# Attention output in eight narrow products side by side, and its row sums through 32x32 transposes on VectorE

## The chip, the cores and the metric

The kernel runs on one core of a Trainium2 chip. The metric is the device time of one launch in microseconds. Before the change it is 1025.22 us, the median of three runs (1023.84 to 1025.31).

The core's engines run beside each other, each through its own queue of instructions: TensorE multiplies matrices, VectorE and ScalarE work elementwise and read what TensorE leaves in PSUM, GpSimd adds, SyncE issues most of the transfers. In the profile TensorE appears as PE (products) and PEld (loading of the stationary operand), VectorE as DVE, ScalarE as ACT, GpSimd as POOL, SyncE as SP.

## What is computed

A linear attention without softmax for 8 batches, 8 heads, 576 tokens and 64 dimensions a head; its output is divided by its root mean square over the 64 dimensions; then follows an MLP with a leaky ReLU on the 4608 x 512 matrix x that the heads side by side make. The weights w_in and w_out are float64 in memory, the rest is float32.

```python
kv  = einsum('bhsd,bhse->bhde', k, v)
out = einsum('bhsd,bhde->bhse', q, kv)
rms = sqrt(mean(out * out, axis=-1, keepdims=True) + 1e-06)
a   = out / rms * g_norm
x   = a.transpose(0, 2, 1, 3).reshape(4608, 512)
h   = x @ w_in                     # 512 x 2048
return maximum(0.01 * h, h) @ w_out  # 2048 x 512
```

## The kernel before

**Order of the work.** The 4608 tokens make nine blocks of 512. Attention goes by batches of 576 tokens, so that each batch falls into two stretches that end at block borders (448 and 128 tokens for batch 1, 384 and 192 for batch 2, up to 64 and 512 for batch 7). `first_attention` (L316) computes kv of batch 0 and its first 512 tokens, in two halves of 256. `first_block` (L515) runs the MLP of block 0 in 16 plain rounds of h (4 products of 512 columns) and o_acc (4 products of 512 columns); between them `between` (L555) starts the rest of batch 0 (64 tokens), the steps of batch 1, and loads and rounds the float64 weights. Then the loop at L570 runs the blocks 1 to 8, each in four chunks of `product_h` (L445) and `product_o` (L478). These are Strassen products: seven products of halves for four quarter results. One of the seven is four matmuls of 256 columns and shows in the trace as a row "x8", since each float32 matmul is two records. After two of the products of each `product_h` and `product_o`, `go(a_steps, 1)` puts in one step of the attention of the next batch: 16 places a block.

**Who sets the order.** TensorE's order is the order of the program (`matmul`, L84, pins each). What SyncE loads and the rounding of weights is pinned too. VectorE and ScalarE get their order from the scheduler of the framework, which puts an instruction where its inputs are ready by its own reckoning; on the chip that order is fixed.

**The attention of one batch** (`attention`, L297). Four steps, one for each pair of heads: q is transposed by VectorE in 32x32 blocks (L303), and kv of both heads of the pair is multiplied into the PSUM tile kv_ps (L250). Then `copy_kv` (L253) copies kv into `kvs`, a tile that was zeroed once (L140): for each pair p and each e of 4 there are 32 columns, 16 of one head and 16 of the other, and the rows of the other head are zero. So one product over 128 rows serves both heads. Then for each stretch four steps of `outputs` (L262) and one of `divide` (L277):

- `outputs` for one e: four products, one for each pair, 128 rows to 32 output rows each, side by side in one PSUM tile o_ps; ScalarE reads it twice, once squared into sq (L270), once times g into x[:, e] (L271); VectorE adds the squares up (L274).
- `divide`: one matmul with `same`, a matrix of ones in 16x16 blocks on the diagonal (L223 to L228), adds the squares over the 16 rows of a head into ss_ps and spreads the sum over them (L280); ScalarE takes the root (L282), VectorE the reciprocal (L283) of all n columns, and multiplies x by it (L284).

The PSUM tiles of these steps come from the pool ps_att with two buffers ("att"). The MLP uses the other six banks as h_a, h_b, h_c, o_a, o_b, o_c. The product that accumulates into a bank waits until VectorE or ScalarE has read it; the closest such pairs have one other product between them: 7 and 4 in `product_h`, 6 and 7 as well as 7 and 4 in `product_o`. VectorE's adds for this are at L373 (`add`).

**The order of rows in x.** Row p of x[:, e] is row 4p + e of the transposed x, so w_in is read as "(p e) f -> p e f" (L191) with one DMA for each piece of 128 columns (L164).

Of the kernel before, what the change touches and what calls it, by code (L numbers as in the profile page):

```python
# [11 lines left out]
AF = mybir.ActivationFunctionType  # L12
ALU = mybir.AluOpType
# [8 lines left out]
def kernel(  # L22
# [27 lines left out]

    nc = tc.nc
# [4 lines left out]
    E = P // H  # L56
# [11 lines left out]
    assert H * D == DM and S == 64 * (J + JJ) and E * NE == D and B * S == NB * NT  # L68
# [89 lines left out]

    def load_f64(src):
        a, n = src.shape[1:]  # L160
        n //= 2
        pool, tag = next(raw_homes)
        raw = pool.tile([P, a * n, 2], U32, tag=tag, name="raw")
        pin(nc.sync.dma_start(raw.rearrange("p (a n) two -> p a (n two)", a=a), src))  # L164
        return raw
# [25 lines left out]
    w_in_e = w_in.rearrange("(p e) f -> p e f", e=NE)  # L191
    w_jobs = []
    for c in range(NC):
        for h in range(2):
            for u in range(U):
                f0 = h * (DF // 2) + (c * U + u) * P
                w_jobs += [(w1_sb[h][c][:, u], w_in_e[:, :, f0:f0 + P]),
                           (w2_sb[h][c][:, u:u + 1, :], w_out[f0:f0 + P].unsqueeze(1))]
# [4 lines left out]
    def load_w(j):  # L203
# [3 lines left out]
        else:  # L207
            nc.sync.dma_start(dst, src)

    def round_w(j):  # L210
        if w_in.dtype == I64:
# [10 lines left out]

    same = consts.tile([P, H, E], F32, name="same")  # L223
    nc.gpsimd.memset(same, 1.0)
    nc.gpsimd.affine_select(same, same, pattern=[[-E, H], [0, E]], base=0, channel_multiplier=1,
                            compare_op=ALU.is_ge, fill=0.0)
    nc.gpsimd.affine_select(same, same, pattern=[[E, H], [0, E]], base=E - 1,
                            channel_multiplier=-1, compare_op=ALU.is_ge, fill=0.0)  # L228


    g_sb = consts.tile([P, NE], F32, name="g_sb")
    for h in range(H):
        pin(nc.gpsimd.dma_start(g_sb[h * E:(h + 1) * E], g_norm.rearrange("(i e) -> i e", e=NE)))

# [18 lines left out]
    def copy_kv(b, ps, kv_ps):  # L253
        for l in range(2):
            r = slice(64 * l, 64 * l + 64)
            nc.vector.tensor_copy(kvs[b % 2][r, ps, :, l, :],
                                  kv_ps[r, ps].rearrange("p a (i e) -> p a e i", e=NE))

    def t2k(n, name):
        return work.tile([P, n], F32, tag="t2k", name=name, bufs=4)  # L260

    def outputs(b, lo, hi, e, sums, o_ps, new=t2k):  # L262

        i, n = lo // NT, hi - lo
        x = block(i)[:, :, lo - i * NT:hi - i * NT]
        for p in range(NP):
            matmul(o_ps[32 * p:32 * p + 32, :], lhsT=kvs[b % 2][:, p, e, :, :],
                   rhs=qTs[b][:, p, lo - b * S:hi - b * S], start=True, stop=True)
        sq = new(n, "sq")
        nc.scalar.activation(sq, o_ps, func=AF.Square)  # L270
        nc.scalar.activation(x[:, e, :], o_ps, func=AF.Copy, scale=g_sb[:, e:e + 1])  # L271
        if sums is None:
            return sq
        nc.vector.tensor_add(sums, sums, sq)  # L274
        return sums

    def divide(lo, hi, sums, ss_ps, new=t2k):  # L277
        i, n = lo // NT, hi - lo
        x = block(i)[:, :, lo - i * NT:hi - i * NT]
        matmul(ss_ps, lhsT=same.rearrange("p h e -> p (h e)"), rhs=sums, start=True, stop=True)  # L280
        rms = new(n, "rms")
        nc.scalar.activation(rms, ss_ps, func=AF.Sqrt, scale=1.0 / D, bias=eps_sb)  # L282
        nc.vector.reciprocal(rms, rms)  # L283
        nc.vector.tensor_mul(x, x, rms.unsqueeze(1).to_broadcast([P, NE, n]))  # L284
# [31 lines left out]
    def first_attention():  # L316
# [4 lines left out]
        def keep_warm(n=1):  # L321
            for _ in range(n):
                matmul(idle, lhsT=kvs[1][:, 0].rearrange("p e l i -> p (e l i)"),
                       rhs=kvs[1].rearrange("p a e l i -> p (a e l i)"), start=True, stop=True)
# [30 lines left out]
        free = iter(("ob", "hb", "hc", "oa", "oc", "ha", "ob", "hb", "hc", "oa"))  # L355

        def ps(name):
            return ps_m.tile([P, N2], F32, tag=next(free), name=name)

        sums = [None, None]  # L360
        for e in range(NE):
            sums[0] = outputs(0, 0, N2, e, sums[0], ps("o_ps"), spare)
        sums[1] = outputs(0, N2, NT, 0, None, ps("o_ps"), spare)
        divide(0, N2, sums[0], ps("ss_ps"), spare)
        for e in range(1, NE):
            sums[1] = outputs(0, N2, NT, e, sums[1], ps("o_ps"), spare)
        divide(N2, NT, sums[1], ps("ss_ps"), spare)
# [183 lines left out]
    steps = {6 + i: tail for tail in [tail_of(0, NT, S)] for i in range(NE + 1)}  # L551
    steps.update((i, a1) for a1 in [attention(1)] for i in (12, 13, 16, 17, *range(18, 29)))
# [73 lines left out]
```

## Time and profile before

| | |
|---|---|
| median of three runs | 1025.22 us |
| the profiled execution | 1025.05 us, its span 1023.3 us |
| mean granted TensorE clock | 0.997 |
| PE busy | 1001.4 us, 98% of the span |
| DVE, ACT, POOL busy | 424.4, 262.6, 505.0 us |
| o_ps products, of 64 to 512 columns | 544 records, 68 steps |
| ss_ps products | 34 records, 17 steps |

The page gives the busy time of each engine, the chain of work that ended last, and the costliest groups of instructions with their mean duration. The timeline lists instructions in order of time, merged where they follow each other: start, length, engine, line, operation, output and inputs, shape, number; in brackets the idle time of the engine before it and what ended it. All matmuls have line L85, the helper; what they do is told by the tile that they write. The end of a matmul is modelled and overlaps the next one, so costs on TensorE are best read from start to start. The waits list says who waited for whom, in total, how often, and the longest.

### The profile page before, as it was taken

The numbers are of one execution on the slowest core, as the hardware profiler recorded it, in microseconds if no ns is written. First come the engines' busy times: TensorE is split into PE (matmuls) and PEld (weight loads), VectorE is DVE, ScalarE is ACT, GpSimd is POOL, SyncE is SP. The second block draws the span as 40 slices with busy tenths as digits, with TensorE's granted clock in tenths as the row PEclk, the third lists the DMA queues.
The fourth block names the chain that finished last, engine by engine and source line by source line (L and its number), as shares of the span: only waits on it lengthen the run. The fifth ranks groups of instructions, "written<-read, shape, count | busy, mean of one in ns | idle before, by whom it ended". The sixth has DMA issues, their size and how long they took to land.

```text
span 1023.3 us, 13007 instructions
## 1 busy us (share of the span) xinstructions
PE 1001.4 (98%) x5164; PEld 773.2 (76%) x5164; DVE 424.4 (41%) x591; ACT 262.6 (26%) x497; POOL 505.0 (49%) x403
## 2 busy tenths in 40 slices
PE   8799999999999999999999999999999999999997
PEld 4444336778887788878888788878887888888886
DVE  2896681235323533156313722354323521332222
ACT  2653432322123211322132212221222112112210
POOL 2000212555655655556555655564555566666641
PEclk9899999999999999999999999999999999999999
DMA  9598404300340016000520043002100010001001
GB/s 226 200 292 224 131 0 125 102 0 1 92 134 1 1 53 174 1 1 1 164 62 1 1 118 108 1 1 76 58 1 1 1 42 1 1 1 42 1 1 41
DMA packets 45309, 63.41 MB, mean 62 GB/s; under 512 B 5312, under 2 KB 39104, under 8 KB 45248
## 3 DMA queue, kind: packets, MB, share of 16 engines
q1 hardware_dynamic: 34560, 51.95, 18.5%
q10 hardware_dynamic: 10432, 10.62, 3.3%
q8 instruction: 41, 0.67, 0.3%
q14 instruction: 20, 0.16, 0.1%
q0 software_dynamic: 256, 0.00, 0.0%
HBM read 53.12 MB, written 9.44 MB: 61 GB/s over the span
## 4 chain that ended last, share of the span: by engine, by line
PE 91%; DVE 4%; DMA 2%; SPq 1%; issue 1%; ACT 0%; DVEq 0%; ACTq 0%
PE o_a L85 21%; PE h_a L85 21%; PE h_c L85 11%; PE o_c L85 10%; PE o_b L85 5%; PE h_b L85 5%; PE h_ps L85 5%; PE o_acc L85 5%; PE o_ps L85 3%; PE kv_ps L85 2%; DVE rms L283 2%; PE ss_ps L85 1%; DMA k_in<-in_k_dram 1%; DVE sq L274 1%; DMA early_kv<-in_v_dram 1%
## 5 line engine op out<-in xcount | busy, mean ns | idle before, releaser
L85 PE MATMUL o_a<-wt,gs 128*128 128x256 f32 x512 | 124.8, 386 | 2.9 <-DVE o L373 2.9
L373 DVE TENSOR_TENSOR o<-o_a,o 128x512 f32<-128x512 f32 x104 | 71.3, 686 | 130.0 <-PE o_a L85 130.0
L373 POOL TENSOR_TENSOR ws<-w 128x512 f32<-128x512 f32 x32 | 44.1, 1377 | 146.7 <-PE h_a L85 98.5
L85 PEld LDWEIGHTS o_a<-wt,gs 128*128 128x128 f32 x512 | 94.1, 190 | 28.5 <-issue 10.4
L373 POOL TENSOR_TENSOR wt<-w,w 128x512 f32<-128x512 f32 x32 | 41.1, 1284 | 150.0 <-PE o_a L85 150.0
L373 POOL TENSOR_TENSOR gs<-g,g 128x512 f32<-128x512 f32 x64 | 82.2, 1284 | 23.3 <-ACT g L452 22.9
L452 ACT ACTIVATE g<-g 128x512 f32<-128x512 f32 x96 | 60.4, 629 | 128.0 <-DVE g L373 127.6
L373 POOL TENSOR_TENSOR ws<-w,w 128x512 f32<-128x512 f32 x32 | 42.5, 1328 | 101.6 <-DMA v_in<-in_v_dram 100.9
L373 POOL TENSOR_TENSOR wt<-w,wt 128x512 f32<-128x512 f32 x64 | 83.0, 1297 | 2.5
L373 POOL TENSOR_TENSOR wt<-w 128x512 f32<-128x512 f32 x32 | 40.9, 1277 | 70.0 <-PE o_a L85 67.2
L373 DVE TENSOR_TENSOR o<-o_c,o 128x512 f32<-128x512 f32 x56 | 38.6, 690 | 85.3 <-PE o_c L85 81.9
L457 ACT COPY g<-h_a 128x512 f32<-128x512 f32 x32 | 18.7, 585 | 198.3 <-PE h_a L85 198.3
L85 PE MATMUL h_a<-xt,w 128*128 128x256 f32 x256 | 61.2, 382 | 3.0 <-DVE g L373 3.0
L373 DVE TENSOR_TENSOR g<-h_b,g 128x512 f32<-128x512 f32 x32 | 22.1, 689 | 101.0 <-PE h_b L85 101.0
L85 PE MATMUL o_a<-wt,g 128*128 128x256 f32 x256 | 60.7, 380 | 1.7 <-DVE o L373 1.7
L85 PE MATMUL h_a<-xT,ws 128*128 128x256 f32 x256 | 62.4, 387 | 0.0
L85 PE MATMUL h_a<-xt,ws 128*128 128x256 f32 x256 | 62.4, 386 | 0.0
L85 PE MATMUL h_ps<-xT,w 128*128 128x512 f32 (+1 forms) x136 | 61.3, 599 | 0.9 <-DVE xT L284 0.9
L85 PE MATMUL o_a<-w,g 128*128 128x256 f32 x256 | 60.6, 379 | 0.8 <-DVE o L373 0.8
L85 PE MATMUL h_a<-xT,w 128*128 128x256 f32 x256 | 60.6, 379 | 0.0
L85 PE MATMUL o_c<-w,gs 128*128 128x256 f32 x256 | 60.5, 379 | 0.0
L85 PE MATMUL h_c<-xT,ws 128*128 128x256 f32 x256 | 60.5, 379 | 0.0
(86 smaller groups left out, 1767.4 us busy)
## 6 DMA issues: line engine op xcount, KB each, us to landing
out_dram<-o ACTq DMA_DIRECT2D x36, 256.0 KB, 2.2
raw<-in_moe_w_in_dram SPq DMA_DIRECT2D x16, 512.0 KB, 5.8
raw<-in_moe_w_out_dram SPq DMA_DIRECT2D x16, 512.0 KB, 6.5
q_in<-in_q_dram SPq DMA_DIRECT2D x56, 144.0 KB, 3.4
q_in<-in_q_dram SPq DMA_DIRECT2D x56, 140.0 KB, 3.4
k_in<-in_k_dram SPq DMA_DIRECT2D x30, 160.0 KB, 3.7
v_in<-in_v_dram SPq DMA_DIRECT2D x30, 160.0 KB, 3.7
k_in<-in_k_dram SPq DMA_DIRECT2D x30, 128.0 KB, 3.5
```

The lines of the kernel that those rows point to most:

```text
L85: pin(nc.tensor.matmul(*args, **kw))
L274: nc.vector.tensor_add(sums, sums, sq)
L283: nc.vector.reciprocal(rms, rms)
L373: eng.tensor_tensor(out_, a, b_, op=ALU.subtract if minus else ALU.add)
L452: nc.scalar.activation(t, t if src is None else src, func=AF.Prelu, alpha=SLOPE)
L457: nc.scalar.copy(g11, bank)
```

## The change

The 64 dimensions of a head are cut into two parts of 32 (E = 32, before four parts of 16). A tile of x holds 32 dimensions of one head of each of the four pairs: x[:, 2l + e] is part e of head l of each pair.

- `outputs` runs for two values of e instead of four. Each takes two PSUM tiles, one for each head l of the pairs, and makes eight products of 64 rows and 32 columns: the head's own rows of kv and q alone, so that kv needs no zeros and is copied by one instruction.
- The row sums are no matmul any more. VectorE transposes the squares in 32x32 blocks, adds over 32 (tensor_reduce), and after root (ScalarE) and reciprocal (VectorE) of n/32 values for each head ScalarE spreads them over 32 columns, VectorE transposes back and multiplies x, for each head by itself.
- A stretch has three steps instead of five: the steps of the attention of a batch need 11 of the 16 places of a block instead of 15. The places in the first block are renumbered.
- The rows of w_in follow the new order of x: "(p t i) f -> p i t f", four DMAs of 32 partitions for each piece.
- keep_warm, which multiplies zeros at the start, uses a tile `zeros` of its own; `same` and its construction are gone; g comes in four small DMAs instead of eight.

```diff
-    E = P // H
+    E = 32
...
-    kvs = []
-    for i in range(2):
-        kv = consts.tile([P, NP, NE, 2, E], F32, name=f"kv_{i}")
-        nc.gpsimd.memset(kv, 0.0)
-        kvs.append(kv)
+    kvs = [consts.tile([P, NP, D], F32, name=f"kv_{i}") for i in range(2)]
+    zeros = gpool.tile([P, NT], F32, tag="g11", name="zeros")
+    nc.gpsimd.memset(zeros, 0.0)
...
+    def load(t, src):
+
+        if len(src.shape) == len(t.shape):
+            t, src = [t], [src]
+        else:
+            n = src.shape[1]
+            t = [t[i * n:(i + 1) * n] for i in range(src.shape[0])]
+        for to, part in zip(t, src):
+            pin(nc.sync.dma_start(to, part))
...
-    w_in_e = w_in.rearrange("(p e) f -> p e f", e=NE)
+    w_in_e = w_in.rearrange("(p t i) f -> p i t f", p=NP, i=E)
...
     def copy_kv(b, ps, kv_ps):
+        nc.vector.tensor_copy(kvs[b % 2][:, ps, :], kv_ps[:, ps, :])
+
+    def t2k(n, name):
+        home = {"tag": name, "bufs": 1} if name[:3] == "sum" else {"tag": "t2k", "bufs": 3}
+        return work.tile([P, n], F32, name=name, **home)
...
+    def outputs(b, lo, hi, e, sums, new_ps, new=t2k):
+        x, n = x_of(lo, hi), hi - lo
+        o_ps = [new_ps(n, "o_ps") for _ in range(2)]
+        for p in range(NP):
+            for l in range(2):
+                r = slice(64 * l, 64 * l + 64)
+                matmul(o_ps[l][E * p:E * p + E, :], lhsT=kvs[b % 2][r, p, E * e:E * e + E],
+                       rhs=qTs[b][r, p, lo - b * S:hi - b * S], start=True, stop=True)
         for l in range(2):
+            sq = new(n, "sq" if e else f"sum{l}")
+            nc.scalar.activation(sq, o_ps[l], func=AF.Square)
+            nc.scalar.activation(x[:, 2 * l + e, :], o_ps[l], func=AF.Copy,
+                                 scale=g_sb[:, e:e + 1])
+            if e == 0:
+                sums.append(sq)
+            else:
+                nc.vector.tensor_add(sums[l], sums[l], sq)
+
+    def divide(lo, hi, sums, new=t2k):
+        x, n = x_of(lo, hi), hi - lo
+        rms = work.tile([P, 2, n // E], F32, tag="rms", name="rms", bufs=2)
+        for l in range(2):
+            t = new(n, "turned")
+            nc.vector.transpose(t, sums[l])
+            nc.vector.tensor_reduce(rms[:, l, :], t.rearrange("p (a i) -> p a i", i=E),
+                                    axis=AX.X, op=ALU.add)
+        nc.scalar.activation(rms, rms, func=AF.Sqrt, scale=1.0 / D, bias=eps_sb)
         nc.vector.reciprocal(rms, rms)
-        nc.vector.tensor_mul(x, x, rms.unsqueeze(1).to_broadcast([P, NE, n]))
+        for l in range(2):
+            t = new(n, "spread")
+            nc.scalar.copy(t.rearrange("p (a i) -> p a i", i=E),
+                           rms[:, l, :].unsqueeze(2).to_broadcast([P, n // E, E]))
+            inv = new(n, "inv")
+            nc.vector.transpose(inv, t)
+            to = x[:, 2 * l:2 * l + 2, :]
+            nc.vector.tensor_mul(to, to, inv.unsqueeze(1).to_broadcast([P, 2, n]))
...
     def tail_of(b, lo, hi):
-        sums = None
-        for e in range(NE):
-            sums = outputs(b, lo, hi, e, sums, att_ps(hi - lo, "o_ps"))
+        sums = []
+        for e in range(2):
+            outputs(b, lo, hi, e, sums, att_ps)
             yield
-        divide(lo, hi, sums, att_ps(hi - lo, "ss_ps"))
+        divide(lo, hi, sums)
         yield
...
+        sums = [], []
+        for e in range(2):
+            outputs(0, 0, N2, e, sums[0], ps, spare)
+        outputs(0, N2, NT, 0, sums[1], ps, spare)
+        divide(0, N2, sums[0], spare)
+        outputs(0, N2, NT, 1, sums[1], ps, spare)
+        divide(N2, NT, sums[1], spare)
...
-    steps = {6 + i: tail for tail in [tail_of(0, NT, S)] for i in range(NE + 1)}
-    steps.update((i, a1) for a1 in [attention(1)] for i in (12, 13, 16, 17, *range(18, 29)))
+    steps = {i: tail for tail in [tail_of(0, NT, S)] for i in (6, 8, 10)}
+    steps.update((i, a1) for a1 in [attention(1)]
+                 for i in (12, 13, 16, 17, 19, 21, 23, 24, 25, 27, 28))
```

More of the change, by code (lines that the diff above doesn't have):

```diff
@@ L12 @@
 AF = mybir.ActivationFunctionType
+AX = mybir.AxisListType
 ALU = mybir.AluOpType
@@ L67 @@
     EPS = 1e-6
-    assert H * D == DM and S == 64 * (J + JJ) and E * NE == D and B * S == NB * NT
+    assert H * D == DM and S == 64 * (J + JJ) and 2 * E == D and NP * E == P and B * S == NB * NT
     assert DM // 2 == N2 and NE == 4
@@ L163, in load_f64 @@
         raw = pool.tile([P, a * n, 2], U32, tag=tag, name="raw")
-        pin(nc.sync.dma_start(raw.rearrange("p (a n) two -> p a (n two)", a=a), src))
+        load(raw.rearrange("p (a n) two -> p a (n two)", a=a), src)
         return raw
@@ L221 @@
                             compare_op=ALU.is_equal, fill=0.0)
[L223 to L233, printed above, removed]
+    g_sb = consts.tile([P, 2], F32, name="g_sb")
+    for p in range(NP):
+        pin(nc.gpsimd.dma_start(g_sb[p * E:(p + 1) * E], g_norm.rearrange("(e i) -> i e", i=E)))
     xTs = {}
@@ L253, in copy_kv @@
     def copy_kv(b, ps, kv_ps):
-        for l in range(2):
[L255 to L284, printed above, removed]
+        nc.vector.tensor_copy(kvs[b % 2][:, ps, :], kv_ps[:, ps, :])
@@ L322, in keep_warm @@
             for _ in range(n):
-                matmul(idle, lhsT=kvs[1][:, 0].rearrange("p e l i -> p (e l i)"),
-                       rhs=kvs[1].rearrange("p a e l i -> p (a e l i)"), start=True, stop=True)
+                matmul(idle, lhsT=zeros[:, :P], rhs=zeros, start=True, stop=True)
         keep_warm(2)
@@ L354, in first_attention, with ps @@
         round_w(0)
[L355 to L367, printed above, removed]
+        free = iter(("ha", "hb", "hc", "oa", "ob", "oc", "ha", "hb"))
+        def ps(n, name):
+            return ps_m.tile([P, n], F32, tag=next(free), name=name)
+        sums = [], []
[5 more added lines that the diff above has]
+        divide(N2, NT, sums[1], spare)
         for j in range(1, 5):
```

9 lines of the change are left out of this document (6 added, 3 removed).

## The prediction, made before the changed kernel had run

> **What bounds the kernel now.** I read the page first (busy shares, then the chain that ended last), then the timeline of TensorE in the middle of the run, then the waits of TensorE, and last the opening 45 us.
>
> ```profile
> PE 1001.4 (98%) x5164; PEld 773.2 (76%) x5164; DVE 424.4 (41%) x591; ACT 262.6 (26%) x497; POOL 505.0 (49%) x403
> PE 91%; DVE 4%; DMA 2%; SPq 1%; issue 1%; ACT 0%; DVEq 0%; ACTq 0%
> ```
>
> TensorE is busy for 98% of the span and carries 91% of the chain; VectorE has 59% of its time free, ScalarE 74%. So a microsecond of matmul taken out of the middle should come out of the total, as long as nothing else makes TensorE wait. What a step costs there is read from start to start in TensorE's timeline (start us, length us, what):
>
> ```profile
> 514.80 1.89 PE L85 MATMUL h_c<-xT,ws 128*128 128x256 f32 x8
> 516.62 0.53 PE L85 MATMUL o_ps<-qT,kv 128*32 128x192 f32 x8
> 517.08 1.99 PE L85 MATMUL h_a<-xT,ws 128*128 128x256 f32 x8
> 518.91 1.89 PE L85 MATMUL o_a<-w,g 128*128 128x256 f32 x8
> 520.64 1.89 PE L85 MATMUL h_a<-xt,w 128*128 128x256 f32 x8
> ...
> 550.57 1.89 PE L85 MATMUL o_b<-w,g 128*128 128x256 f32 x8
> 552.39 0.85 PE L85 MATMUL o_ps<-qT,kv 128*32 128x384 f32 x8
> 553.17 1.99 PE L85 MATMUL o_a<-wt,gs 128*128 128x256 f32 x8
> 555.00 1.89 PE L85 MATMUL o_c<-w,gs 128*128 128x256 f32 x8
> ...
> 578.72 1.89 PE L85 MATMUL o_b<-w,g 128*128 128x256 f32 x8
> 580.44 0.81 PE L85 MATMUL ss_ps<-sq,same 128*128 128x384 f32 x2
> 581.09 1.89 PE L85 MATMUL o_a<-wt,gs 128*128 128x256 f32 x8
> 582.81 1.89 PE L85 MATMUL o_c<-w,gs 128*128 128x256 f32 x8
> 585.21 1.97 PE L85 MATMUL o_a<-wt,gs 128*128 128x256 f32 x8 [0.50 <-DVE o L373]
> ```
>
> An MLP product of eight records takes 520.64 - 518.91 = 1.73 us. An o step of 192 columns in between costs 518.91 - 514.80 - 2 x 1.73 = 0.65 us, one of 384 columns 555.00 - 550.57 - 3.46 = 0.97 us. The difference is 0.32 us for 192 columns, 1.67 ns a column, and 0.33 us of each o step does not depend on the columns. The row-sum matmul of 384 columns costs 582.81 - 578.72 - 3.46 = 0.63 us, which is 384 x 1.67 ns with no constant. Two things follow. The four o products of a step (x8, two records each) take as long as one product of the full 128 columns, so four products of 32 output columns do run side by side. And the constant belongs to the change of shape (128*128 to 128*32 and back), which the row-sum matmul does not make.
>
> **The change, part by part.**
>
> *The o products (outputs).* A batch has 576 columns in two stretches. Before: four steps a stretch, so 8 x 0.33 + 4 x 576 x 1.67 ns = 2.64 + 3.85 = 6.49 us, and the row sums 576 x 1.67 ns = 0.96 us: 7.45 us a batch. After: two steps a stretch, each of eight 64x32 products. If eight run side by side, a step still costs 1.67 ns a column, so the columns cost 2 x 0.96 = 1.92 us, and the row-sum matmul is gone. The constant of a step is unknown for this shape: at least the 0.33 us of four products, at most double that, 0.66 us, if it grows with the products. I take 0.40, close to the lower end, because the row-sum matmul, whose x2 records pay no constant, shows that it is the shape and not the product that costs. After: 4 x 0.40 + 1.92 = 3.52 us. Saved: 3.93 us a batch, 27.5 us for the seven batches from 1 to 7 (4.21 us a batch at 0.33, 2.89 at 0.66). The 64 columns of batch 0 that are left to the first block save 4 x (0.33 + 0.11) + 0.11 - 2 x (0.40 + 0.11) = 0.85 us. Together 28.3 us. No o product of 64 rows in the upper half stands in this trace, so side-by-side running of the two row halves is the assumption here that nothing shows; the first rival prices its failure.
>
> A rule speaks against this packing. The Trainium skill, "TensorE: Matmul & The Clock Gate", Part 3, says that matmuls start and end strictly in program order; eight products whose two records each share a place would then queue up one behind the other. By that rule four products of two records would take five halves of 1.67 ns a column, 4.2 ns; this trace shows 1.67 for all four. The same mechanism, priced from the rows, is the third rival.
>
> *The division (divide), on VectorE and ScalarE.* The row sums leave TensorE for VectorE: per stretch two 32x32 transposes, two sums over 32, two transposes back, and on ScalarE two spreading copies; the reciprocal shrinks from n columns to n/16.
>
> ```profile
> L303 DVE STREAM_TRANSPOSE qT<-q_in 128x576 f32<-128x576 f32 x28 | 34.8, 1248 | 1.6 <-DMA q_in<-in_q_dram 1.1 <-PE o_ps L85 0.4
> L373 DVE TENSOR_TENSOR o<-o_c,o 128x512 f32<-128x512 f32 x56 | 38.6, 690 | 85.3 <-PE o_c L85 81.9 <-issue 3.1
> L452 ACT ACTIVATE g<-g 128x512 f32<-128x512 f32 x96 | 60.4, 629 | 128.0 <-DVE g L373 127.6
> ```
>
> ```profile
> 802.79 3.35 DVE L283 RECIPROCAL rms<-rms 128x512 f32<-128x512 f32 x1 [0.95 <-ACT rms L282]
> 806.06 0.63 DVE L373 TENSOR_TENSOR o<-o_a,o 128x512 f32<-128x512 f32 x1
> 806.60 2.28 DVE L284 TENSOR_TENSOR xT<-xT,rms 128x2048 f32<-128x2048 f32 x1
> ```
>
> At 512 columns a transpose is 1248 x 512/576 = 1.11 us if the strided one of q is the measure; a dense one may be as short as an add, 0.69 us. The trace has no sum over 32; the nearest row is the add, 0.69 us. So VectorE does 4 x 1.11 + 2 x 0.69 + about 0.1 + 2.28 = 8.2 us (6.5 us with short transposes) where it did 3.35 + 2.28 = 5.6 us, and one add less (0.69). That is at most 1.9 us more per 512 columns, some 17 us over 4608, in 424 us of busy time on an engine with 59% free: nothing by itself. The spreading copies are 2 x 0.63 us on ScalarE. What counts is whether TensorE waits.
>
> ```profile
> PE o_a L85 <- DVE o L373: 5.4, 6, 1.4
> PE h_a L85 <- DVE g L373: 3.0, 5, 0.8
> ```
>
> ```profile
> 806.83 1.97 PE L85 MATMUL o_a<-wt,gs 128*128 128x256 f32 x8 [1.41 <-DVE o L373]
> ```
>
> All of TensorE's waits for VectorE are 8.4 us, and the longest, 1.41 us, ends when the add that had queued behind the 3.35 us reciprocal is done at 806.69. A long instruction that cannot be cut is what hurts. After, the longest is about 1.2 us, and adds can slip in between, as the one at 806.06 did between reciprocal and multiply. Against that stand more steps, and two places where VectorE waits for ScalarE (square root, spread) with the adds of the products queued behind. I let these waits fall from 8.4 to 6.0 us, a gain of 2.4; the bounds are a gain of 5 and a loss of 5.
>
> *Two PSUM tiles a step.* Both att tiles are taken at once, so the next step's products wait until ScalarE has read both: at 512 columns four readings of about 0.63 us, 2.5 us, beside 0.63 for an activation. Two o steps lie two products apart, 3.46 us. That holds; if it did not at the widest stretches, tenths of a microsecond each, inside the bounds above.
>
> *The opening.* Here nothing hides a delay.
>
> ```profile
> 23.41 3.04 PE L85 MATMUL o_ps<-qT,kv 128*32 128x256 f32 x40
> 27.88 0.67 PE L85 MATMUL ss_ps<-sq,same 128*128 128x256 f32 x2 [1.43 <-DVE sq L274]
> 28.48 1.50 PE L85 MATMUL o_ps<-qT,kv 128*32 128x256 f32 x24
> 33.27 0.67 PE L85 MATMUL ss_ps<-sq,same 128*128 128x256 f32 x2 [3.28 <-DVE sq L274]
> 33.77 2.86 PE L85 MATMUL h_ps<-xT,w 128*128 128x256 f32 x8
> 37.55 7.30 PE L85 MATMUL h_ps<-xT,w 128*128 128x256 f32 x16 [0.91 <-DVE xT L284]
> ```
>
> ```profile
> 34.00:38.00 4.00, 3.09 (x9) 2.05 (x8) 3.45 (x4) 4.00 (x8) 0.00 (x0) 0.57 0.36 118
> ```
>
> (In the second row the 0.57 is the granted clock.) The first half of x no longer waits behind the second half's sums, so its h products should start some 2 us before 33.77. The second half decides: from its last sum on, two transposes (0.55 each at 256 columns), two sums (0.35 to 0.4), root, reciprocal and spread (about 1), then twice a transpose and 0.6 of multiply make about 5.2 us, where 33.27 to 37.55 is 4.3 us, and part of it queues behind the first half's chain on VectorE. I call it even, between 2 us earlier and 2.5 us later. The clock adds to that: after the 3.28 us of waiting it was granted at 0.57. With one longer idle stretch in place of two it would be low about as long.
>
> *Weights and small things.* w_in now comes in four DMAs a piece.
>
> ```profile
> 15.81 1.28 SPq L164 DMA_DIRECT2D raw<-in_moe_w_in_dram  x2
> ...
> 84.82 1.93 SPq L111 DMA_DIRECT2D q_in<-in_q_dram  x4
> ```
>
> One issue was 0.64 us, four issues of 32 partitions each (the q loads) 1.93, so 1.3 us more of SyncE per piece, 21 us over 16 pieces, spread over the first block; behind them in the queue stand w_out and the k, v and q of batch 1. The first piece is wanted only by the h products near 33 us. Cover gone, it is 1 to 2 us, once, inside the opening's bounds. Half as many copies of kv, and one memset in place of two, are worth tenths.
>
> *Sum.* 28.3 + 2.4 + 0 = 30.7 us. The profiled execution took 1025.05 us (span 1023.3 and 1.75 around it), 0.17 below the median of 1025.22: 1025.05 - 30.7 = 994.3, so 994 us.
>
> **The rivals.**
>
> 1. *The two row halves do not run side by side*, and a step of eight costs twice 1.67 ns a column. For it: no row shows it done. Against: the output columns do it four at a time, and the halves write to different PSUM tiles. A batch costs 4 x 0.40 + 3.85 = 5.45 us, saving 2.0; seven make 14.0, batch 0's rest 0.6, waits 2.4: 1008 us.
>
> 2. *VectorE's longer chain becomes TensorE's wait: slower.* If the whole chain of a divide ran with no add between, it would hold the adds for 8.2 us and about 1 us of ScalarE at 512 columns, against a slack of two products less the add, 2.8 us: a wait of 6.4 us. With about 16 ns a column and 1 us, the fourteen divides of batches 1 to 7 (64 to 512 columns, 4032 in all) wait 40 us together. In place of the old 8.4 us: 1025 - 28.3 - 8.4 + 40 = 1028 us. It decides the sign from (28.3 + 8.4) / 14 = 2.6 us of wait a divide on. Against it: the add at 806.06.
>
> 3. *Strict order of start.* Sixteen records in a row, each pair in one place, would take nine halves of 1.67 ns a column: 7.5 ns a column, 10.2 us a batch, 2.8 us more than before; with the waits falling by 2.4, about 1043 us. Against it: four products in 1.67 ns a column, where it would want 4.2.
>
> 4. *The gain is given back* to the opening and to waits, within 2 us of 1025.
>
> **How the numbers follow.** Forecast 0.76, rival 1 0.14, rival 2 0.05, rival 3 0.02, rival 4 0.03. The forecast's own range: constants of 0.33 or 0.66 move it by -2 or +7, waits by -3 or +7, the opening by -2 or +2.5, seldom all one way: 987 to 1004. The range reaches to rival 1: 986 to 1010. Faster by over 0.2%, 2 us, about what can be told from no change: 0.90; slower 0.07; same 0.03.
>
> **What would show it.** In the changed profile: o steps of x16 records whose cost from start to start rises by 1.67 ns a column (3.3 is rival 1, 7 rival 3), with a constant near 0.4 us; no ss_ps rows; no RECIPROCAL over 0.2 us; TensorE's waits for VectorE near 6 us in all (over 34 is rival 2); the opening's sixteen h_ps records ending near 44.9 us (37.55 + 7.30), as before. If the total is right and these are not, the prediction was right by accident.

## The result and the profile after

After the change the kernel takes 998.58 us (median of four runs, 998.06 to 999.84); before, beside it, 1025.24 us. The ratio is 0.9745, with an interval of 0.9728 to 0.9762: 26.7 us less, where 30.7 were forecast. The profiled execution took 998.52 us, 26.5 us less than that of before; its span is 996.7 us. One run of sums_by_matmul (1621 us, at a granted clock of 0.60) and one of far_pairs (1688 us, at 0.56) are left out of the times given below.

The page: busy shares, and the chain that ended last.

```profile
PE 970.3 (97%) x5130; PEld 766.5 (77%) x5130; DVE 435.6 (44%) x682; ACT 268.1 (27%) x531; POOL 500.7 (50%) x395
PE 83%; DVE 4%; DMA 2%; SPq 1%; ACT 1%; issue 1%; DVEq 0%
```

TensorE is busy 31.1 us less and the span is 26.6 us shorter, so about 4.5 us went into idle time of TensorE. VectorE has 11.2 us more work, not 17. TensorE's timeline at the second stretch of batch 5 and at the first of batch 6, the ones shown of before:

```profile
501.52 1.89 PE L87 MATMUL h_c<-xT,ws 128*128 128x256 f32 x8
503.34 0.56 PE L87 MATMUL o_ps<-qT,kv 64*32 64x192 f32 x16
...
505.66 1.89 PE L87 MATMUL o_a<-w,g 128*128 128x256 f32 x8
...
528.47 1.89 PE L87 MATMUL h_c<-xT,ws 128*128 128x256 f32 x8
530.29 0.88 PE L87 MATMUL o_ps<-qT,kv 64*32 64x384 f32 x16
...
532.93 1.89 PE L87 MATMUL o_a<-w,g 128*128 128x256 f32 x8
535.80 1.56 PE L87 MATMUL h_a<-xt,w 128*128 128x256 f32 x6 [0.98 <-DVE g L388]
```

From start to start, less two products of 1.73 us, an o step costs 505.66 - 501.52 - 3.46 = 0.68 us at 192 columns and 532.93 - 528.47 - 3.46 = 1.00 at 384: 1.67 ns a column and a constant of 0.36. So all eight products run side by side. The last row, which the view cuts short, is new: product 4 of product_h waits 0.98 us for an add of VectorE. The waits of TensorE for VectorE in the blocks 1 to 8:

```profile
PE h_a L87 <- DVE g L388: 7.8, 7, 2.1
PE o_a L87 <- DVE o L388: 2.7, 4, 0.9
```

Together 10.5 us, before 8.4, forecast 6.0. The 7.8 us are one wait a block, always before product 4: 0.78 us in block 1 (0.79 in before), then 2.11, 0.93, 0.96, 0.98, 1.01 and 1.01. The new operations of VectorE, grouped:

```profile
L289 DVE STREAM_TRANSPOSE turned<-sum 128x512 f32<-128x512 f32 x2 | 1.4, 704 | 0.0
L290 DVE TENSOR_REDUCE rms<-turned 128x16 f32<-128x512 f32 x2 | 1.4, 678 | 0.0
L293 DVE RECIPROCAL rms<-rms 128x16 f32<-128x16 f32 (+7 forms) x17 | 4.4, 257 | 5.9 <-ACT rms L292 5.9
```

A dense transpose of 512 columns is 0.70 us, the lower of the two bounds. The opening, and the waits of the first block, which before had one of 0.73 us:

```profile
31.35 3.75 PE L87 MATMUL h_ps<-xT,w 128*128 128x256 f32 x8 [4.53 <-DVE xT L301]
36.37 7.28 PE L87 MATMUL h_ps<-xT,w 128*128 128x256 f32 x16 [1.27 <-ACT cut L192]
...
100.22 0.95 PE L87 MATMUL kv_ps<-v_in,k_in 128*64 128x64 f32 x20 [0.91 <-DMA v_in<-in_v_dram]
...
146.72 3.70 PE L87 MATMUL h_ps<-xT,w 128*128 128x512 f32 x8 [0.78 <-DVE w L199]
151.90 1.52 PE L87 MATMUL o_acc<-w,gT 128*128 128x512 f32 x3 [1.48 <-DVE w L199]
```

```profile
148.47 0.46 PE L85 MATMUL ss_ps<-sq,same 128*128 128x128 f32 x2 [0.73 <-DVE sq L274]
```

The sixteen h_ps records start 37.55 - 36.37 = 1.2 us earlier than before; the first block has waits of 0.91 + 0.78 + 1.48 = 3.2 us. The balance of the two profiled runs: a batch's o steps cost 4 x 0.36 + 1.92 = 3.36 us in place of 7.45, so 7 x 4.09 = 28.6 us, and 0.9 for the rest of batch 0; plus 1.2 of the opening; less 10.5 - 8.4 = 2.1 of waits, less 3.2 - 0.7 = 2.4 in the first block: 26.2 of the 26.5 us measured.

### The profile page after: what moved, and what is told of

Same layout as the page of the kernel before. It is cut to its first block, busy times and chain, and to the rows that moved or that the text cites. A ratio compares the mean times of both kernels' runs of the same rounds, so it can differ in the third digit from the quotient of the medians.

```text
span 996.7 us, 13085 instructions
## 1 busy us (share of the span) xinstructions
PE 970.3 (97%) x5130; PEld 766.5 (77%) x5130; DVE 435.6 (44%) x682; ACT 268.1 (27%) x531; POOL 500.7 (50%) x395
## 4 chain that ended last, share of the span: by engine, by line
PE 83%; DVE 4%; DMA 2%; SPq 1%; ACT 1%; issue 1%; DVEq 0%
PE o_a L87 21%; PE h_a L87 21%; PE h_c L87 11%; PE o_c L87 11%; PE o_b L87 6%; PE h_b L87 6%; PE o_acc L87 2%; PE kv_ps L87 2%; PE h_ps L87 2%; PE o_ps L87 2%; DVE qT L320 1%; DVE sum L282 1%; DMA v_in<-in_v_dram 1%; DMA k_in<-in_k_dram 1%; DVE g L388 0%
## 5 line engine op out<-in xcount | busy, mean ns | idle before, releaser
L87 PE MATMUL o_a<-wt,gs 128*128 128x256 f32 x512 | 122.6, 382 | 0.0
L87 PEld LDWEIGHTS h_a<-xt,w 128*128 128x128 f32 x256 | 48.1, 190 | 16.9 <-DVE g L388 10.6
L388 DVE TENSOR_TENSOR g<-h_c,g 128x512 f32<-128x512 f32 x32 | 22.1, 692 | 88.9 <-PE h_c L87 88.9
```

Of the source, the lines that this page charges most:

```text
L87: pin(nc.tensor.matmul(*args, **kw))
L388: eng.tensor_tensor(out_, a, b_, op=ALU.subtract if minus else ALU.add)
```

## The experiments

All times are medians unless said otherwise, and each ratio is to the kernel before on the same chip. The kernel after stands at 998.6 us and 0.9745. Two questions were open: which part of the change gives the gain, and where the two losses (the waits before product 4, those of the first block) come from.

**The two row halves one after the other** (one_half).

```diff
-                r = slice(64 * l, 64 * l + 64)
+                r = slice(0, 64)
```

> The changed kernel, but the products of both heads of a pair read rows 0 to 63 of kv and q, so that no product uses the upper half of the rows (the second head's output is left out, the first's is computed twice). Theory, the two row halves run side by side: now they cannot, a step costs 3.33 ns a column instead of 1.67, 1.92 us more a batch, 13.4 us over batches 1 to 7 and up to 2 us in the opening: 1012 to 1014 us. Rival, the halves queue up in the changed kernel too and the gain comes from elsewhere: no change, 998.6 us.

Measured 1009.9 us, ratio 0.9864 [0.9846, 0.9882]: 11.4 us more than the kernel after, 2 us below the range of the theory. Its timeline of TensorE:

```profile
507.22 1.89 PE L87 MATMUL h_c<-xT,ws 128*128 128x256 f32 x8
509.04 0.87 PE L87 MATMUL o_ps<-qT,kv 64*32 64x192 f32 x16
...
511.67 1.89 PE L87 MATMUL o_a<-w,g 128*128 128x256 f32 x8
...
535.44 1.89 PE L87 MATMUL h_c<-xT,ws 128*128 128x256 f32 x8
537.26 1.51 PE L87 MATMUL o_ps<-qT,kv 64*32 64x384 f32 x16
...
540.53 1.89 PE L87 MATMUL o_a<-w,g 128*128 128x256 f32 x8
```

A step costs 0.99 and 1.63 us here: 3.33 ns a column, twice that of the kernel after, and a constant of 0.35. So the overlap of the halves is worth 1.92 us a batch, 13.4 us in the seven batches; 1.7 us of it are given back by shorter waits before product 4 (6.1 us in all where the kernel after has 7.8), which is most of why the total grew by less. The first rival of the prediction is settled: this is how it would have looked, and the kernel after does not look so.

**The row sums through transposes, in the kernel before** (sums_alone). The narrow products are left out; the four tiles of x stay as they were. Root and reciprocal are of n/16 columns.

```diff
-        matmul(ss_ps, lhsT=same.rearrange("p h e -> p (h e)"), rhs=sums, start=True, stop=True)
...
+        nc.vector.transpose(t, sums)
+        nc.vector.tensor_reduce(rms, t.rearrange("p (a i) -> p a i", i=E),
+                                axis=AX.X, op=ALU.add)
...
+        nc.vector.transpose(inv, t)
+        nc.vector.tensor_mul(x, x, inv.unsqueeze(1).to_broadcast([P, NE, n]))
```

> The kernel before with the other part alone: o in four products with zeros as before, the row sums by VectorE's 32x32 transposes (sums over 16 rows). Theory: the row-sum matmul of 0.96 us a batch is gone, 6.8 us with batch 0's rest, and waits within 3 us either way: 1016 to 1021 us. Rival, the longer chain on VectorE costs TensorE more in waits than the matmul did: 1025 us or more.

Measured 1012.3 us, ratio 0.9877 [0.986, 0.9894]: 12 us less than before, more than either case gave (the theory's range began at 1016). The waits of TensorE:

```profile
PE o_a L86 <- DVE o L382: 2.5, 3, 0.9
PE h_a L86 <- DVE g L382: 2.2, 3, 0.8
PE o_c L86 <- DVE o L382: 1.2, 2, 0.9
```

The row-sum matmuls give 7 x 0.96 = 6.7 us, the waits fall from 8.4 to 5.9, and the opening's sixteen h_ps records start at 34.96, 2.6 us before the 37.55 of the kernel before: 11.8 us. The profiled run was the shortest of the four (1010.2 us), and its span is 14.8 us below that of before; the 3 us between are not taken apart here. Taking the long reciprocal off VectorE is worth what the prediction took it for: it had put the waits at 6.0. What raises them to 10.5 must come with the narrow products and the places of their steps.

**The narrow products with the row sums by matmul** (sums_by_matmul).

```diff
-            nc.vector.transpose(t, sums[l])
...
+            matmul(ss_ps, lhsT=same.rearrange("p h e -> p (h e)"), rhs=sums[l],
+                   start=True, stop=True)
...
+            nc.scalar.activation(rms, ss_ps, func=AF.Sqrt, scale=1.0 / D, bias=eps_sb)
+            nc.vector.reciprocal(rms, rms)
```

> The narrow products alone: x tiles and eight products as in the changed kernel, the row sums by a matmul with ones in 32x32 blocks, one for each head of the pairs, and a reciprocal of all columns. Theory, TensorE's time decides: two matmuls of 576 columns more a batch, 1.92 us, 13.4 us for seven batches, and 0 to 6 us of waits behind reciprocals of up to 3.35 us, two a stretch: 1012 to 1020 us. Rival, the row sums on VectorE were nearly all of the gain: 1023 us or more.

Measured 1065.3 us, ratio 1.0418 [1.0351, 1.0486]: 45 us above the range of the theory. The number falls under the rival's "1023 us or more", but not for the rival's reason. The expectation had counted two reciprocals of n columns a stretch, one for each head of the pairs, and put the waits behind them at 0 to 6 us; TensorE's waits for VectorE in the blocks are 43.1 us (35.3 before products that write o_a, 7.8 before those that write h_a). VectorE's timeline at the divide of batch 7, and TensorE's there and at an earlier divide (475.20):

```profile
810.71 6.57 DVE L298 RECIPROCAL rms<-rms 128x512 f32<-128x512 f32 x2 [0.89 <-ACT rms L297]
817.20 2.29 DVE L300 TENSOR_TENSOR xT<-xT,rms 128x1024 f32<-128x1024 f32 x2
819.40 0.68 DVE L387 TENSOR_TENSOR o<-o_a,o 128x512 f32<-128x512 f32 x1
```

```profile
475.20 1.97 PE L87 MATMUL o_a<-wt,gs 128*128 128x256 f32 x8 [3.13 <-DVE o L387]
...
812.38 1.89 PE L87 MATMUL o_c<-w,gs 128*128 128x256 f32 x8
820.23 3.75 PE L87 MATMUL o_a<-wt,gs 128*128 128x256 f32 x8 [5.96 <-DVE o L387]
823.78 2.56 PE L87 MATMUL h_a<-xT,w 128*128 128x256 f32 x8
```

The add of o_a stands behind 6.57 us of reciprocals and two multiplies, and TensorE waits 5.96 us. After that it runs at half speed: 3.75 us for a product of 1.97, in a stretch where the granted clock was 0.50. This is the second rival's mechanism, as a measurement: the chain holds the adds, and the price is the wait and the slow stretch behind it. The kernel after has no such row: a reciprocal of both heads takes 0.18 us (stretch of 64) to 0.35 us (stretch of 512). What TensorE's row-sum products alone would cost, which the run was to show, it does not show.

**w_in by one DMA a piece** (w_in_one_dma).

```diff
-    w_in_e = w_in.rearrange("(p t i) f -> p i t f", p=NP, i=E)
+    w_in_e = w_in.rearrange("(p e) f -> p e f", e=NE)
```

> The changed kernel with each piece of w_in loaded by one DMA in the old order of rows (the rows of w_in then do not belong to those of x; the order is left out). Theory, the four issues a piece delay loads in the first block: its three waits of 0.91, 0.78 and 1.48 us for v and for rounded weights go, 995 to 996 us. Rival, the weights are rounded late because the divides stand ahead of them on ScalarE and VectorE: 998 us or more, with the waits still there.

Measured 995.4 us, ratio 0.9714 [0.97, 0.9729], as expected: 3.2 us less, and the three waits of the first block are gone. The last loads of weights on SyncE's queue, in the kernel after and here:

```profile
117.86 1.79 SPq L167 DMA_DIRECT2D raw<-in_moe_w_in_dram  x4
119.81 1.00 SPq L167 DMA_DIRECT2D raw<-in_moe_w_out_dram  x2
```

```profile
105.45 0.57 SPq L167 DMA_DIRECT2D raw<-in_moe_w_in_dram  x1
106.12 1.04 SPq L167 DMA_DIRECT2D raw<-in_moe_w_out_dram  x2
```

Four issues take 1.79 us where one takes 0.57, and with all pieces the last load leaves SyncE 12 to 14 us later. But the load itself is not what TensorE waits for at the end of the first block. The last issue ends at 120.8 us, and by the page's 5.7 us from issue to landing (an estimate) its data is there by about 127. ScalarE begins to round the last three pieces only at 143.03, behind its spreading copies for a divide of batch 1; with one DMA it begins them at 131.7.

```profile
143.03 0.67 ACT L190 ACTIVATE add<-raw 128x512 uint32<-128x512 uint32 x1
```

VectorE is done with the first two of them at 146.7 and 151.8 us, where the two waits end. Three of its instructions between take 1.37, 1.64 and 1.64 us where the same ones just before take 0.43, 0.69 and 0.69; GpSimd's adds begin beside them at 146.6. The run shows that the four DMAs are the cause. That they act by the place which the rounding gets in the fixed order of ScalarE and VectorE fits these rows and is not tested by itself.

**Pairs of heads p and p + 4** (far_pairs). This is a correct layout with fewer DMAs: two for each piece of w_in, over all 128 partitions.

```diff
-        hs = slice(2 * p, 2 * p + 2)
+        hs = slice(p, None, NP)
...
-    w_in_e = w_in.rearrange("(p t i) f -> p i t f", p=NP, i=E)
+    w_in_e = w_in.rearrange("(l p e) f -> p l e f", l=2, e=2)
...
-                matmul(o_ps[l][E * p:E * p + E, :], lhsT=kvs[b % 2][r, p, E * e:E * e + E],
+                matmul(o_ps[l][E * p:E * p + E, :], lhsT=kvs[b % 2][r, p, e::2],
```

> Changed against the kernel after: a pair is made of heads p and p + 4 instead of 2p and 2p + 1, and part e of a head is its dimensions 2i + e; w_in then needs two DMAs of 128 partitions for each piece instead of four of 32. All of the computation is kept. Theory: the three waits of the first block (0.91, 0.78, 1.48 us) come from the time that SyncE takes for each issue: two take about 1.28 us, four 1.93, one 0.64, so half of the delay is gone and about half of the 3.2 us that one DMA saved: 996 to 997.5. Rival: it is the number of partitions of a DMA that counts, and two with all 128 partitions are as good as one: 995 to 995.7.

Measured 993.9 us, ratio 0.9703 [0.969, 0.9717]: as good as one DMA, below the 996 to 997.5 of my theory. The loss is not halved but gone, and in the trace of far_pairs_earlier (below), with the same loads, none of the three waits is left. That it is the partitions of each DMA, as the rival had it, isn't shown by that; a cover that two issues do not use up gives the same time.

**The transposes of q in program order** (q_pinned). In the kernel after, two transposes of q for the next batch stand in front of the add for which product 4 waits. Here each is pinned to its place.

```diff
-            nc.vector.transpose(
+            pin(nc.vector.transpose(
```

> The changed kernel with the transposes of q kept in the place that the program gives them, so that they no longer run right behind a batch's last o step on VectorE. Theory, these two transposes of 1.25 us are what holds the add that product 4 of h waits for in each block (0.78 to 2.11 us, 7.8 us in all): most of it goes, 991 to 994 us. Rival, the divide's own chain holds the add: its instructions move up into the same place and the waits stay, 997 us or more.

Measured 1023.5 us, ratio 0.999: a miss, for a reason beside the point. In the first block the pinned transposes, the roundings and the loads hold each other up; TensorE's timeline:

```profile
115.26 1.53 PE L87 MATMUL kv_ps<-v_in,k_in 128*64 128x64 f32 x20 [14.70 <-DMA v_in<-in_v_dram]
...
139.44 2.79 PE L87 MATMUL o_ps<-qT,kv 64*32 64x448 f32 x8 [6.11 <-DVE qT L320]
```

From block 2 on, though, the run answers its question. The waits before product 4 are 1.15, 1.25, 0.94, 0.97, 1.00 and 1.02 us with no transpose of q in front of the add: only the 2.11 of block 2 fell, and the 0.93 of block 3 rose. In their place the two adds of squares have grown: ahead of the 1.15 us wait they take 1.31 and 1.01 us for 192 columns. The transposes of q are not the cause.

**The second stretch later** (last_at_h2). Three empty places before a batch's second stretch, from batch 2 on, so that other steps come before product 7.

```diff
         for i in (b, b + 1):
+            if i > b > 1:
+                for _ in range(3):
+                    yield
             yield from tail_of(b, max(i * NT, b * S), min((i + 1) * NT, (b + 1) * S))
```

> The changed kernel with three empty places ahead of the second stretch of batches 2 to 7, so that a batch's last o step follows the product 2 of h in place of the product 3, and VectorE has four products of time instead of two before TensorE needs its next add. Theory, what VectorE does behind the last o step (transposes of q or divide) is only late by a microsecond or two: the waits of product 4 go, 991 to 994 us. Rival, VectorE or ScalarE is short of time in that part of the block altogether: the waits move to another product, 997 us or more.

Measured 997.2 us, ratio 0.973 [0.9716, 0.9743]: above the range of the theory. The waits did not move to another product, as the rival had it. Those before product 4 fell to 4.7 us, but one of them is now 1.86 us, and the product behind it takes 3.66 us in place of 1.97. TensorE's row, and a row of VectorE's timeline ahead of it:

```profile
242.67 3.66 PE L87 MATMUL h_a<-xt,w 128*128 128x256 f32 x8 [1.86 <-DVE g L391]
```

```profile
236.32 2.23 DVE L282 TENSOR_TENSOR sum<-sum,sq 128x192 f32<-128x192 f32 x2
```

Two adds of 192 columns in 2.23 us, where one took 0.35 us in the mean in the kernel before. From there on VectorE is busy up to the add that TensorE waits for, with that stretch's divide in between. In the kernel after, VectorE and GpSimd look so ahead of the 0.98 us wait:

```profile
531.30 1.26 DVE L320 STREAM_TRANSPOSE qT<-q_in 128x576 f32<-128x576 f32 x1
532.40 1.19 DVE L282 TENSOR_TENSOR sum<-sum,sq 128x384 f32<-128x384 f32 x1
533.51 1.25 DVE L320 STREAM_TRANSPOSE qT<-q_in 128x576 f32<-128x576 f32 x1
534.61 0.54 DVE L282 TENSOR_TENSOR sum<-sum,sq 128x384 f32<-128x384 f32 x1
535.08 0.67 DVE L388 TENSOR_TENSOR g<-h_a,g 128x512 f32<-128x512 f32 x1
```

```profile
531.90 1.27 POOL L388 TENSOR_TENSOR gs<-g,g 128x512 f32<-128x512 f32 x1 [0.56 <-ACT g L467]
533.18 1.56 POOL L388 TENSOR_TENSOR ws<-w,w 128x512 f32<-128x512 f32 x1
```

The first add of squares starts while GpSimd's add (531.90 to 533.17) runs, and ends at 533.59, 0.42 us after it; the second, which begins 0.1 us before GpSimd's next add ends, takes 0.54. The transposes beside the same GpSimd adds keep their 1.25 us. The Trainium skill, "SBUF — State Buffer", section "SBUF: two separate sides", says that VectorE and GpSimd share one pair of ports which is locked for a whole instruction, and that an instruction of VectorE with two SBUF inputs waits for it while GpSimd reads SBUF. These rows agree: the add takes its turn behind the whole add of GpSimd. All twelve adds of squares of the kernel after that start during an add of GpSimd end later than it, by 0.21 us at 192 columns up to 0.55 us at 512; the 28 transposes of q take 1.22 to 1.26 us, beside such an add or not. The same add in before and after, grouped by shape:

```profile
L274 DVE TENSOR_TENSOR sq<-sq 128x192 f32<-128x192 f32 x6 | 2.1, 354 | 0.5 <-ACT sq L270 0.2
```

```profile
L282 DVE TENSOR_TENSOR sum<-sum,sq 128x192 f32<-128x192 f32 x4 | 3.4, 864 | 0.1
```

In the kernel after both adds of a stretch come with one o step, and that step lies right before product 7, when GpSimd begins its adds for the next chunk. Two experiments test this: more time for VectorE, and no such adds.

**The steps one product earlier** (steps_earlier). In product_h the steps come after products 5 and 6 instead of after products 2 and 3.

```diff
-                if n in (1, 3):
+                if n in (0, 2):
```

> Changed against the kernel after: in product_h a step of the attention comes after products 5 and 6 instead of after products 2 and 3, so that two products, not one, lie between an o step and product 4, which waits for the add of product 7. Theory: the wait before product 4, once a block (7.0 us in the seven blocks from 1 to 7 in the kernel after: 0.78, 2.11, 0.93, 0.96, 0.98, 1.01, 1.01), comes from VectorE's sums of an o step, which wait for ScalarE's squares and stand ahead of that add; with 1.73 us more for them the waits fall to 1 to 2 us, and the time from 998.6 to 992.5 to 994. Rival: whatever stands there (transposes of q, sums, divides) moves along and holds another add as long, or ScalarE's copy for product 7 comes late behind the squares: the wait changes its name, and the time stays at 997 or above.

Measured 996.1 us, ratio 0.9719 [0.9706, 0.9732]. The five runs go from 993.3 to 996.8 us; the profiled one is that of 993.3, so its trace shows the waits and not the whole of the time. In it the waits before product 4 went from 7.8 to 3.9 us and those before o_a from 2.7 to 3.5, together from 10.5 to 7.4: partly gone, neither the 1 to 2 of the theory nor the rival's mere change of name. The longest is 1.0 us. (The 7.0 us of the expectation are the blocks 2 to 7; with block 1 it is 7.8.)

**No adds of squares** (no_sum_adds). Each tile of squares is turned and summed by itself; one small reduction joins the two parts.

```diff
...
-                nc.vector.tensor_add(sums[l], sums[l], sq)
...
+            t = new(n, "turned")
+            nc.vector.transpose(t, sq)
+            nc.vector.tensor_reduce(sums[0][:, l, e, :], t.rearrange("p (a i) -> p a i", i=E),
+                                    axis=AX.X, op=ALU.add)
...
+        nc.vector.tensor_reduce(rms, sums[0].rearrange("p l e a -> p l a e"),
+                                axis=AX.X, op=ALU.add)
```

> Changed against the kernel after: no add of two SBUF tiles stands between an o step and the root. Each tile of squares is turned and summed over 32 by itself, and the two parts are joined by one small reduction; VectorE gets two transposes and two sums more for each divide and two adds less, about 1.2 us more of work at 384 columns. All of the computation is kept. Theory: the waits before product 4 (7.0 us in blocks 1 to 7 of the kernel after) come from the adds of squares that start while an add of GpSimd runs and end only 0.2 to 0.4 us after that one (1.19 us for 384 columns where the next takes 0.54; the excess is 2.05, 0.87, 0.76, 0.66 us in the first four such blocks); transposes and reductions do not show it. The waits before product 4 fall to 1.5 to 2.5 us in all and the time from 998.6 to 993 to 995, although VectorE has more to do. Rival: it is the amount of VectorE work ahead of the add that counts; with 1.2 us more the waits grow by up to 1 us a block, and the time is 999 to 1005.

Measured 996.6 us, ratio 0.9727 [0.9714, 0.9741]. VectorE's busy time rose from 435.6 to 447.0 us, and the wait for it fell; TensorE's waits:

```profile
PE h_ps L87 <- DVE xT L300: 5.5, 1, 5.5
PE h_a L87 <- DVE g L387: 3.6, 6, 0.9
```

The waits before product 4 in the blocks from 2 on fell from 7.0 to 2.8 us (0.39, 0.31, 0.51, 0.71, 0.91 and none). VectorE had more to do and TensorE waited less, so the adds themselves cost the time, and the rival, which gave 999 or more, is out. The total gained only 2 of these 4 us. In the profiled run the sixteen h_ps records of the opening start at 38.90 us in place of 36.37. Ahead of them TensorE waited 3.0 us for loads of q where the kernel after has 0.8, which the edit does not touch, and 5.5 us for x where it has 4.53, which is the longer chain. The rest of the first block is 1.1 us shorter, and from block 1 on the run is 3.5 us shorter.

**Together.** Three combinations of the edits above, all of them with the whole computation.

The pairs p and p + 4 with the earlier steps (far_pairs_earlier):

> Both edits together, with all of the computation: the pairs of heads p and p + 4 with two DMAs for each piece of w_in, and the steps after products 5 and 6 of product_h. Theory: the two waits lie in different blocks, so the gains add up: about 990 to 992. Rival: the steps of the second block start from another state and the gains overlap: 994 or more.

991.6 us, ratio 0.9679 [0.9666, 0.9692], as expected: the two losses lie in different blocks.

The pairs with no adds of squares (no_adds_far_pairs):

> The edit without the adds of squares together with pairs of heads p and p + 4 (two DMAs for each piece of w_in instead of four). All of the computation is kept. Theory: the waits before product 4 and those of the first block are separate, so the gains add up: 989 to 991. Rival: as for the edit alone, the longer work of VectorE takes back what the missing adds give: 994 or more.

992.0 us, ratio 0.9683 [0.967, 0.9696]: 1 us above the range of the theory. The wait for x in the opening is 5.5 us here too, 1.0 us longer than in the kernel after; that this is the whole of the difference is not shown, as the five runs go from 990.5 to 993.4 us.

All three (no_adds_far_earlier):

> The same two edits, and the steps after products 5 and 6 of product_h instead of 2 and 3. All of the computation is kept. Theory: if the adds of squares were the cause, little is left for the earlier places to take away: within 2 us of the kernel without them, 988 to 991. Rival: the earlier places and the missing adds each take away another part of the waits: 2 to 4 us below the kernel without the earlier places.

987.9 us, ratio 0.9647 [0.9633, 0.966], the best of all kernels here, 10.6 us below the kernel after. It is 4.0 below the one without the earlier steps: here the rival was right. Without the adds of squares the waits before product 4 fell from 7.8 to 3.6 us, with the earlier places from 7.8 to 3.9, and with both to 1.1: each takes away about half, and neither is the whole cause. TensorE's waits for VectorE in the blocks are down to 3.8 us:

```profile
PE o_a L87 <- DVE o L391: 2.7, 4, 0.9
PE h_a L87 <- DVE g L391: 1.1, 2, 0.8
```

## Why the prediction was right, and where it was off

The mechanism was right: TensorE bound the kernel, the products that were removed lay on its path, and all eight products of a step run side by side. Forecast 30.7 us of gain, measured 26.5. That the two are so near is in part luck: the o products and the opening gave 1.2 us each more than forecast, the waits and the DMAs of w_in 4.5 and 2.4 less. By its steps:

- **The o products**, 28.3 us: measured 28.6 + 0.9 = 29.5. The slope was 1.67 ns a column as assumed, the constant 0.36 and not 0.40. The assumption on which nothing in the trace stood, that the row halves overlap, held; one_half measures what its failure would have cost. Strict order of start, the third rival, would have shown 7.5 ns a column; the trace shows 1.67. What the prediction concluded from the rule of the Trainium skill, that each pair of records would queue up, does not show here.
- **TensorE's waits for VectorE**, a gain of 2.4: measured a loss of 2.1. This is the step that failed most, by 4.5 us, though inside its bounds of 5 either way. The reasoning on the reciprocal was right, and so was its worth (sums_alone: 8.4 to 5.9). What it did not look at is which step would stand in the place before product 7, and that an add of two SBUF tiles there takes its turn behind GpSimd's adds. The trace of before had that cost in few places (three adds of squares took 1.36 to 1.51 us), with a mean of 354 ns for 192 columns where the kernel after has 864. The prediction also calls 8.4 us all of TensorE's waits for VectorE; that holds from block 1 on, and the trace of before has 5.4 us more before ss_ps and 0.9 before h_ps, nearly all of them in the opening.
- **The four DMAs of w_in**, put at 1 to 2 us inside the opening's bounds: measured 3.2 us, in the first block. The 21 us of SyncE's time were counted and so was what is queued behind; the step that failed is taking "over the first block" as cover. Three waits came behind it: one for a load of v, and two, at 146 to 152 us, for weights that were probably loaded some 15 us before and not yet rounded.
- **The opening**, called even: 1.2 us earlier. The first half of x started its products 2.4 us earlier, as forecast, and the second half decided, as forecast. The view names a rounding (ACT cut, done at 36.28) as the end of its wait of 1.27 us, but VectorE's multiplies of x end the chain of the second half there as well:

```profile
35.58 1.25 DVE L301 TENSOR_TENSOR xT<-xT,inv 128x512 f32<-128x512 f32 x2
```

The first of the two is done at 36.23, and the products start at 36.37. From the last add of squares (done at 32.48) to the second multiply (36.83) the chain took 4.35 us where the prediction had 5.2. The clock was low for longer, not "about as long": it was granted at 0.50 for 10.2 us (29.9 to 40.1) where before it was for 6.8 (34.5 to 41.3). After the wait of 4.53 us eight records took 3.75 us where before they took 2.86; the sixteen behind them took 7.28 and 7.30.
- **The transposes**: 0.70 us at 512 columns, the lower bound; the sum over 32 was 0.68, next to the 0.69 of the add that stood for it.
- **RECIPROCAL under 0.2 us**: wrong, 0.26 us in the mean. It takes 0.18 us for 4 columns and 0.35 for 32, so some 0.15 us of it does not depend on the columns; nothing hung on it.
- **The second rival**, VectorE's chain as TensorE's wait, did not come, as no divide of the kernel after holds an add for long; sums_by_matmul shows that it comes at once when VectorE has 6.6 us of reciprocals in a row.

## What to carry to other kernels

Products that fill only a part of TensorE's array can be put side by side in both directions, by rows and by columns, and a change of shape cost 0.33 us a visit with four products and 0.36 with eight, so count visits and columns. Where work moves to an engine with much free time, the sum of its work says little: look at what will stand in front of the one instruction that TensorE waits for, and whether it reads two SBUF tiles while GpSimd adds. Four DMAs in place of one cost 3.2 us here and two cost nothing that shows, so of added DMAs ask when the last piece behind them is wanted, and where its next step stands in the order.

## What the runs showed of the hardware

- Eight products of 64 rows by 32 columns, into two PSUM tiles, take 1.67 ns a column together, as four of 128 by 32 and one of 128 by 128 do.
- An add of two SBUF tiles on VectorE that starts during an add of GpSimd ends 0.2 us (192 columns) to 0.55 us (512) after that one (1.19 us at 384 columns, where free ones take 0.52 to 0.56); transposes and sums over 32 beside the same adds show no such delay. Three adds of the kernel before that start less than 0.1 us after GpSimd's keep their length (0.34 to 0.55 us), and GpSimd's take 1.5 to 1.7 us in place of 1.27.
- A dense 32x32 transpose costs 0.70 us for 512 columns, the strided one of q 1.25 for 576.
- After a wait of 5.96 us TensorE ran at a granted clock of 0.50, and a product took 3.75 us in place of 1.97. The length of the wait alone does not decide it: after 3.13 us in the same kernel a product took 1.97, after 1.86 us in last_at_h2 one took 3.66. Nor is the length of the slow stretch fixed: after the wait of 4.5 us in the opening the granted clock was 0.50 for 3.4 us in w_in_one_dma, 6.8 in steps_earlier and 10.2 in the kernel after.
